# Retention and an ELU feed-forward network: units of 128 tokens of all heads in place of 256 tokens of four heads

## The chip, the cores and the metric

The kernel runs on one core of a Trainium2 chip. The metric is the device time in microseconds (us). Before the change the median of three runs is 307.68 us (306.76 to 308.19).

## The reference

Two layers follow each other. The first is retention: attention without a softmax, in which the score of a query for an earlier key is multiplied by a power of a decay that belongs to the head. The second is a feed-forward network with an ELU between its two products.

```python
# q, k, v: 8 batches, 8 heads, 576 tokens, 64 features, float32
scores = scale * np.matmul(q, k.transpose(0, 1, 3, 2))      # scale = 1 / 8
gamma  = 1.0 - 2.0 ** (-5.0 - np.arange(H))                 # one decay per head
rel    = pos[:, None] - pos[None, :]
Dmat   = np.where(rel >= 0, gamma ** rel, 0.0)              # causal
attn   = np.matmul(scores * Dmat, v)

x = attn.transpose(0, 2, 1, 3).reshape(8 * 576, 512)
h = x @ w_in                                                # 512 -> 2048
g = np.where(h > 0, h, np.exp(np.minimum(h, 0)) - 1)
out = g @ w_out                                             # 2048 -> 512, float32
```

Since `gamma ** (i - j)` is `gamma ** i * gamma ** -j`, the decay goes into q and k as a factor for each token and head, and the sum over all earlier tokens can be carried as a state, `k.T @ v`, a 64x64 block for each head.

## The kernel before, in words

**Units.** The first 512 tokens of a batch are worked in units, named by `seq` (L154): batch `b`, half `T` of 256 tokens, group `w` of four heads. That is 32 units, four to a batch. A tile holds two neighbouring tokens to a partition, so that a load's pieces are 512 bytes: `"h (p e) d -> p h (e d)"` with `e=2` (L167). The last 64 tokens of each batch go as a *rider* beside a unit (the functions whose name ends in `_rider`); a rider has one token to a partition and its loads (L379, L381) have pieces of 256 bytes.

**One unit.** `load` (L161) issues three DMAs from SP's queue. `cast` (L183) multiplies q and k by their factors, `gq` and `gk`, and turns them into bf16 (`cast_qk`, L178; `cast_v`, L181), mostly on POOL, that is GpSimd. `turn` (L202) transposes q and k by a DMA of SP's queue. Then come, all on PE with instructions that are recorded at L65:

- `scores` (L236): 16 matmuls on 64x64 quarters of the array, 128 columns each, into the PSUM tile `sc`. The two chunks `c` of a tile are 128 tokens each (64 partitions of two tokens).
- `masks` (L249): one DVE instruction that takes `sc` to bf16 and zeroes what isn't causal, into `pt` (L255).
- `inter` (L270): the states `s_first` and `s_mid`, as blocks for a pair of heads, times the queries, on the whole array, 128 columns each; four matmuls, or two in a first half, where no state is there for the first chunk.
- `values` (L280): 16 matmuls on 64x64 quarters, 128 columns each, into the PSUM tiles `x0` and `x1`.
- `state` (L305): 16 matmuls on 64x64 quarters, 64 columns each, into a free part of `x0` and `x1`.
- `prefix_mid` and `prefix_end` (L343, L348): two DVE instructions that add the chunk's state to the sum so far (L321, L323), and four POOL copies that put these sums as bf16 into `s_mid`, `s_first` or `s_last` (L355).
- `put_x` (L291): two ACT copies of the result into `xt`, the input of the feed-forward network (L297).

**Order.** Instructions keep the program's order on each engine (`pin`). `stretch(u)` (L432) works the unit's matmuls, and `inter`, `values` and `put_x` of the unit before it. The feed-forward network goes in jobs: `ffn1_half` (L514), eight matmuls of 256 columns, then on ACT an exponential and a Relu (L495, L498) and on DVE their combination (L499); and `ffn2` (L534), four matmuls of 512 columns, with a copy on ACT (L542) and a store from POOL's queue (L552) after the last four of a tile of tokens. `stage` (L789) runs these jobs in turn and calls `step` (L656) at places that are spread evenly over them. Each step casts and turns unit `u + 2`, loads unit `u + 4`, and works `stretch(u)`. The first eight units, the loads of the weights and the way into this order are written out by hand (L568 to L770).

Of the kernel before, what the change touches and what calls it, by code (L numbers as in the profile page):

```python
# [17 lines left out]
def kernel(  # L18
# [9 lines left out]
    nc = tc.nc  # L28
# [89 lines left out]
    s_mid = [const.tile([P, 2, P], BF16, name=f"s_mid{w}") for w in range(2)]  # L118
    s_first = [const.tile([P, 2, P], BF16, name=f"s_first{w}") for w in range(2)]
    s_last = [[const.tile([P, 2, P], BF16, name=f"s_last{o}{w}") for w in range(2)] for o in range(3)]  # L120
    for t in (*s_mid, *s_first, *s_last[0]):
        nc.vector.memset(t, 0.0)

    w_in_sb = const.tile([P, KJ, DF], BF16, name="w_in_sb")
# [36 lines left out]
    def load(u, last=False):  # L161
        b, T, w = seq[u]
        rqk = raw.tile([P, 2, 4, 2, D], FP32, name="rqk", tag="rqk")
        rv = raw.tile([P, 4, 2, D], FP32, name="rv", tag="rv", bufs=5)
        parts = [(rqk[:, 0], q), (rqk[:, 1], k), (rv, v)]
        for dst, src in parts[::-1] if last else parts:
            pin(nc.sync.dma_start(  # L167
                dst.rearrange("p h e d -> p h (e d)"),
                src[b, 4 * w : 4 * w + 4, 2 * P * T : 2 * P * (T + 1), :].rearrange("h (p e) d -> p h (e d)", e=2),
            ))  # L170
        rawt[u] = rqk, rv

    def cast_qk(u, i, eng, es=(0, 1)):
        b, T, w = seq[u]
        x = rawt[u][0][:, i].rearrange("p h e d -> p e h d")
        g = (gq, gk)[i][:, 2 * T : 2 * T + 2, 4 * w : 4 * w + 4].unsqueeze(3).to_broadcast([P, 2, 4, D])
        for e in es:
            pin(tt[eng](natt[u][0][:, i, e], x[:, e], g[:, e], ALU.mult))  # L178
# [54 lines left out]
    def half(i):  # L233
        return slice(i * D, (i + 1) * D)

    def scores(u):  # L236
        sc = ps_s.tile([P, 2, 512], FP32, name="sc", tag="sc")
        for hl in range(2):
            for ek in range(2):
                for i in range(2):  # L240
                    r = half(i)
                    for c in range(2):
                        cs = slice(c * C, (c + 1) * C)
                        o = (hl * 2 + ek) * P
                        mm(pairs(sc[cs, i, o : o + P]), trt[u][r, 4 + ek * 2 + hl, cs], queries(u, r, hl, c),
                           start=True, stop=True)
        score_ps[u] = sc

    def masks(u, hls=None):  # L249
        sc = score_ps[u]  # L250
        if u not in ptt:
            ptt[u] = ppool.tile([P, 2, 2, 2 * P], BF16, name="pt", tag="pt")
        m = mask.rearrange("p k e r -> p (k e r)").unsqueeze(1)
        if hls is None:
            pin(nc.vector.tensor_tensor(  # L255
                ptt[u].rearrange("p i h n -> p (i h) n"), sc.rearrange("p i (h n) -> p (i h) n", h=2),
                m.to_broadcast([P, 4, 2 * P]), ALU.mult,
            ))
        else:
            for hl in hls:  # L260
                pin(nc.vector.tensor_tensor(
                    ptt[u][:, :, hl], sc.rearrange("p i (h n) -> p i h n", h=2)[:, :, hl],
                    m.to_broadcast([P, 2, 2 * P]), ALU.mult,
                ))
# [5 lines left out]
    def inter(u, hls=(0, 1), to=None):  # L270
        b, T, w = seq[u]
        x = to or xps
        for c in range(2):
            if T + c == 0:
                continue
            s = s_mid[w] if c else s_first[w]
            for hl in hls:
                acc_x(c, 2, pairs(x[c][:, hl * P : (hl + 1) * P]), s[:, hl], queries(u, slice(0, P), hl, c), to)

    def values(u, hls=(0, 1), to=None):  # L280
        vn, pt = natt[u][1], ptt[u]
        x = to or xps
        for hl in hls:
            for e in range(2):
                for c in range(2):
                    cs = slice(c * C, (c + 1) * C)
                    for i in range(2):
                        acc_x(c, i, x[c][half(i), hl * P : (hl + 1) * P], vn[cs, 2 * hl + i, e],
                              pt[cs, i, hl, e * P : (e + 1) * P], to)

    def put_x(u, hls=(0, 1), to=None, eng="ss"):  # L291
        b, T, w = seq[u]
        h0, h1 = hls[0], hls[-1] + 1
        for c in range(2):
            src = (to or xps)[c][:, : 2 * P].rearrange("p (h e r) -> p h e r", h=2, e=2)[:, h0:h1]
            dst = xt_tile(b)[:, T, 2 * w + h0 : 2 * w + h1, c * P : (c + 1) * P].rearrange("p h (r e) -> p h e r", e=2)
            pin(engines[eng[c]](dst, src))  # L297
# [6 lines left out]

    def state(u, to=None):  # L305
        qkn, vn = natt[u]
        stt[u] = to or list(xps)
# [17 lines left out]
    def prefix(u, c, put):  # L325

        b, T, w = seq[u]
        before = mids[u] if c else total[w] if T else None
        new = rpool.tile([P, 2, D], FP32, name="end" if c else "mid", tag="end" if c else "mid")
# [12 lines left out]

    def prefix_mid(u, put="p"):  # L343
        prefix(u, 0, put)
# [15 lines left out]
    def put_end(u, eng="p"):  # L360
        blocks(s_end(u), total[seq[u][2]], eng)


    mask_t = const.tile([P, ST], BF16, name="mask_t")

    def mask_rider():
        pin(nc.vector.memset(mask_t, 1.0))
        for i in range(2):
            m = mask_t[half(i)]
            pin(nc.gpsimd.affine_select(out=m, in_=m, compare_op=ALU.is_ge, fill=0.0, base=0, pattern=[[1, ST]],  # L370
                                        channel_multiplier=-1))

    rawr, natr, trr, ptr, late = {}, {}, {}, {}, []

# [57 lines left out]
    def stretch(u, put="p"):  # L432
        old = u - 1 in natt and u - 1 in ptt
        rider = late.pop() if late else None
        new_x()
        if old:
            inter(u - 1)
        if rider is not None:
            inter_rider(rider)
        if u < NS:  # L440
            scores(u)
            masks(u)
# [6 lines left out]
        if u < NS:  # L449
            state(u)  # L450
        if old:
            put_x(u - 1)
            drop(u - 1)
        if rider is not None:
            put_rider(rider)
        if u < NS:
            prefix_mid(u, put)
            prefix_end(u, put)
        if u in rides:
            masks_rider(rides[u])  # L460
            late.append(rides[u])
# [111 lines left out]
    warm(7)  # L573
    cast(0, "v", "p", None)
    turn_pe(0, between=2)
    warm(2)
    cast(1, "v", "p", None)
    for u in range(FT - 1):
        scores(u)
        cast_v(u, "s")  # L580
        if u == 2:
            cast_v(3, "s")
        if u:
# [15 lines left out]
        if u == 1:  # L599
            cast(3, None, None, None)  # L600
            masks(1)
            turn_pe(2, "ss")
            prefix_mid(1)
            prefix_end(1)
            for t in (*s_last[1], *s_last[2]):
# [159 lines left out]
    finish(7)  # L765
    cast(10)
    turn(10)
    mask_rider()
    while half1:
        some()  # L770
    def mix(a, c):
# [82 lines left out]
```

## Time and profile before

| | |
|---|---|
| median of three runs | 307.68 us |
| lowest, highest | 306.76, 308.19 us |
| profiled execution | 306.73 us |
| its span (first to last instruction) | 305.0 us |
| mean granted clock of PE | 0.999 |
| busy: PE, ACT, POOL, DVE | 297.2, 212.5, 169.5, 165.2 us |
| DMA, mean over the span | 178 GB/s |

The profile is of one execution, and times in it count from the first instruction. A row of the timeline gives start, duration, engine, line of the kernel, operation, output and inputs, and how many neighbouring instructions it merges; the bracket behind it is the idle time of the engine before it and what ended that. A row of the grouped lines ends in busy time, mean duration in ns, and idle time before. In a row of stretches of time, the last three columns are the granted clock, the mean busy share of the 16 DMA engines, and the rate. That share counts a packet's whole time, so packets that overlap on an engine take it above 1. Matmuls are pipelined: the modelled end of one lies behind the start of the next, so the spacing of starts tells what each occupies.

### The profile page before, as it was taken

Reading aid. Unit: us, or ns where it says so; the run is one execution under the profiler, and the core shown is the slowest. Engines: PE = TensorE matmul, PEld = TensorE weight load, DVE = VectorE, ACT = ScalarE, POOL = GpSimd, SP = SyncE. Lnnn points to the kernel's source line nnn. Section 1 sums busy time; section 2 is a strip of 40 time slices with the busy share of each in tenths; the row PEclk is TensorE's granted clock in tenths of the full one; section 3 lists DMA queues with packets and bytes.
Section 4 is the critical chain, followed back from the end, with each engine's and each line's share of the span. In section 5 each row is a group of like instructions: output and inputs, shape, how many; then the busy total and the mean of one; then the engine's idle time right before and its main releaser. Section 6 shows DMA issues by size and latency. Waiting matters only on the chain.

```text
span 305.0 us, 8990 instructions
## 1 busy us (share of the span) xinstructions
PE 297.2 (97%) x3562; PEld 200.4 (66%) x3562; DVE 165.2 (54%) x306; ACT 212.5 (70%) x429; POOL 169.5 (56%) x373
## 2 busy tenths in 40 slices
PE   8889999999999999999999999999999999999995
PEld 5544457767766766777676676677766776666654
DVE  4866566667465556555653455555555555434430
ACT  4679857967766776677777677767776777677751
POOL 5888887787957575757370437584757530201000
PEclk9999999999999999999999999999999999999999
DMA  7999997999999888776944098667759301100112
GB/s 205 315 368 368 356 297 170 258 242 289 264 219 222 216 193 206 195 183 108 263 125 139 34 189 169 172 175 214 172 137 218 88 34 38 38 34 37 49 57 69
DMA packets 102187, 54.34 MB, mean 178 GB/s; under 512 B 46272, under 2 KB 95680, under 8 KB 102144
## 3 DMA queue, kind: packets, MB, share of 16 engines
q1 hardware_dynamic: 99392, 45.04, 63.2%
q0 software_dynamic: 2672, 8.65, 7.6%
q8 instruction: 28, 0.46, 0.6%
q14 instruction: 15, 0.12, 0.1%
q10 hardware_dynamic: 80, 0.07, 0.1%
HBM read 36.70 MB, written 9.44 MB: 151 GB/s over the span
## 4 chain that ended last, share of the span: by engine, by line
PE 82%; DMA 10%; SPq 3%; ACT 1%; DVE 1%; issue 1%; POOL 0%; DVEq 0%
PE pm L65 37%; PE ph L65 36%; DMA rqk<-in_moe_w_out_dram 5%; PE x L65 5%; PE sc L65 3%; SPq L167 3%; DMA rqk<-in_q_dram 2%; DMA rqk<-in_moe_w_in_dram 2%; PE pe L65 1%; DVE pt L255 1%; ACT ph L498 1%; SPq L145 1%; ACT e L495 1%; PE ptr L212 0%; DVE g L499 0%
## 5 line engine op out<-in xcount | busy, mean ns | idle before, releaser
L499 DVE SCALAR_TENSOR_TENSOR g<-e,ph 128x512 bf16<-128x512 f32 x128 | 88.0, 688 | 103.9 <-ACT ph L498 101.3
L65 PEld LDWEIGHTS <-w_in_sb 128*128 128x128 bf16 x1088 | 105.1, 98 | 42.6 <-DVE xt L297 0.5
L65 PE MATMUL pm<-w_out_sb,g 128*128 128x512 bf16 x512 | 131.9, 379 | 0.0
L65 PE MATMUL ph<-xt,w_in_sb 128*128 128x256 bf16 (+1 forms) x960 | 131.4, 280 | 0.1
L495 ACT ACTIVATE e<-ph 128x512 f32<-128x512 f32 x144 | 85.9, 596 | 58.4 <-PE ph L65 58.2
L498 ACT ACTIVATE ph<-ph 128x512 f32<-128x512 f32 x144 | 85.6, 594 | 0.0
L65 PEld LDWEIGHTS <-g 128*128 128x128 bf16 x512 | 48.7, 98 | 35.3
L355 POOL CAST s_mid<-mid 64x128 bf16<-64x128 f32 x64 | 18.6, 291 | 68.6 <-DVE mid L323 38.5
L552 POOL DMA_DIRECT2D out_dram<-ot x35 | 20.0, 574 | 37.5 <-ACT ot L542 31.1
L178 POOL TENSOR_TENSOR qkn<-rqk,gk 128x256 bf16<-128x256 f32 x64 | 37.8, 609 | 4.1 <-DMA rqk<-in_k_dram 3.7
L255 DVE TENSOR_TENSOR pt<-sc,mask 128x1024 bf16<-128x1024 f32 x30 | 36.5, 1218 | 0.7 <-PE sc L65 0.5
L178 POOL TENSOR_TENSOR qkn<-rqk,gq 128x256 bf16<-128x256 f32 x51 | 30.2, 610 | 2.5 <-DMA rqk<-in_q_dram 0.8
L297 ACT CAST xt<-x 128x256 bf16<-128x256 f32 x62 | 23.6, 454 | 9.6 <-PE x L65 9.4
L542 ACT COPY ot<-pm 128x512 f32<-128x512 f32 x35 | 20.5, 589 | 9.5 <-PE pm L65 9.0
L499 DVE SCALAR_TENSOR_TENSOR gt<-e,ph 128x512 bf16<-128x512 f32 x16 | 11.0, 688 | 14.8 <-ACT ph L498 14.8
L65 PE MATMUL ph<-xtail,w_in_sb 128*128 128x256 bf16 x128 | 16.6, 273 | 0.0
L181 POOL CAST vn<-rv 128x512 bf16<-128x512 f32 x23 | 13.9, 602 | 0.0
L65 PE MATMUL sc<-qkT 64*64 64x128 bf16 x512 | 13.3, 222 | 0.0
L65 PE MATMUL x<-pt,vn 64*64 64x128 bf16 x496 | 12.3, 217 | 0.0
L65 PE MATMUL pm<-w_out_sb,gt 128*128 128x512 bf16 x48 | 11.8, 379 | 0.0
L355 POOL CAST s_first<-end 64x128 bf16<-64x128 f32 x32 | 9.9, 311 | 1.7
L65 PEld LDWEIGHTS <-qkT 64*64 64x64 bf16 x512 | 8.2, 106 | 4.1 <-ACT qkT L213 0.9
(77 smaller groups left out, 190.6 us busy)
## 6 DMA issues: line engine op xcount, KB each, us to landing
rqk<-in_q_dram SPq DMA_DIRECT2D x32, 256.0 KB, 3.9
rqk<-in_k_dram SPq DMA_DIRECT2D x32, 256.0 KB, 4.5
rv<-in_v_dram SPq DMA_DIRECT2D x32, 256.0 KB, 5.1
out_dram<-ot POOLq DMA_DIRECT2D x31, 256.0 KB, 3.9
rqk<-in_moe_w_in_dram SPq DMA_DIRECT2D x16, 256.0 KB, 5.7
rqk<-in_moe_w_out_dram SPq DMA_DIRECT2D x16, 256.0 KB, 5.6
rqt<-in_q_dram SPq DMA_DIRECT2D x8, 128.0 KB, 4.8
rqt<-in_k_dram SPq DMA_DIRECT2D x8, 128.0 KB, 5.0
```

The source lines that it names most:

```text
L65: pin(nc.tensor.matmul(*a, **kw))
L167: pin(nc.sync.dma_start(dst.rearrange("p h e d -> p h (e d)"), src[b, 4 * w : 4 * w + 4, 2 * P * T : 2 * P * (T + 1), :].rearrange("h (p e ...
L178: pin(tt[eng](natt[u][0][:, i, e], x[:, e], g[:, e], ALU.mult))
L181: pin(engines[eng](natt[u][1], rawt[u][1]))
L255: pin(nc.vector.tensor_tensor(ptt[u].rearrange("p i h n -> p (i h) n"), sc.rearrange("p i (h n) -> p (i h) n", h=2), m.to_broadcast([P, 4, ...
L297: pin(engines[eng[c]](dst, src))
L355: pin(engines[eng](dst[half(i), :, half(i)], src[half(i)]))
L495: pin(nc.scalar.activation(e, ph, AF.Exp))
L498: pin(nc.scalar.activation(ph, ph, AF.Relu))
L499: pin(nc.vector.scalar_tensor_tensor(dst, view(e), -1.0, view(ph), ALU.add, ALU.min))
L542: pin(nc.scalar.copy(ot, pm))
L552: pin((queue or nc.gpsimd).dma_start(dst, src))
```

## The change

From the third batch on (`fine(u)`, 24 units) a unit is 128 tokens of all eight heads, one token to a partition. The number of units stays: `t = u % 4` names the quarter of the 512 tokens. The two chunks of a unit are 64 tokens each.

- The loads bring pieces of 256 bytes, one head and token each (`"h p d -> p h d"`).
- `cast_qk` is one instruction of 512 elements for q and one for k, with tables of their own, `gqf` and `gkf`, that `tables()` makes at the start, together with `mask_t`, which was made later before. `cast_v` moves behind the stretch.
- `scores` and `values` are 16 matmuls each, of 64 columns; `inter` has one for each of four head pairs and each chunk, of 64 columns. `state` writes into the free half of `sc`, right behind `scores`.
- `masks` is one instruction of 512 elements. The states are added in two instructions of 256 elements (`prefix_fine`) and copied to bf16 by two POOL instructions, which take both chunks at once. At a batch's last unit these two take one chunk, and two more go to `s_last`.
- `s_mid` and `s_first` become parts of one tile, `s_fine[0]`, beside a second, `s_fine[1]`.

The core of the diff:

```diff
+    s_fine = [const.tile([P, 2, HP, P], BF16, name=f"s_fine{o}") for o in range(2)]
+    s_mid, s_first = [[s_fine[0][:, n, 2 * w : 2 * w + 2] for w in range(2)] for n in range(2)]
...
+    def fine(u):
+        return seq[u][0] >= 2
...
     def load(u, last=False):
+        if fine(u):
+            t = u % 4
+            for dst, src in parts:
+                pin(nc.sync.dma_start(
+                    dst.rearrange("p a e d -> p (a e) d"), src[b, :, t * P : (t + 1) * P, :].rearrange("h p d -> p h d"),
+                ))
...
     def cast_qk(u, i, eng, es=(0, 1)):
+        if fine(u):
+            pin(tt[eng](
+                natt[u][0][:, i].rearrange("p e h d -> p (e h) d"), rawt[u][0][:, i].rearrange("p a e d -> p (a e) d"),
+                (gqf, gkf)[i][:, u % 4].unsqueeze(2).to_broadcast([P, H, D]), ALU.mult,
+            ))
...
+    fines = [(m, i, c) for m in range(HP) for i in range(2) for c in range(2)]
     def scores(u):
+        if fine(u):
+            for m, i, c in fines:
+                cs, r = half(c), half(i)
+                mm(sc[cs, i, m * C : (m + 1) * C], trt[u][r, HP + m, cs], trt[u][r, m, cs],
+                   start=(m == 0), stop=True, skip_group_check=True)
...
     def masks(u, hls=None):
+        if fine(u):
+            pin(nc.vector.tensor_tensor(
+                ptt[u], sc[:, :, : HP * C].rearrange("p i (m n) -> p i m n", m=HP),
+                mask_t.unsqueeze(1).unsqueeze(1).to_broadcast([P, 2, HP, C]), ALU.mult,
+            ))
...
     def inter(u, hls=(0, 1), to=None):
+        if fine(u):
+            for c in range(2):
+                if u % 4 + c == 0:
+                    continue
+                s = s_fine[u % 2][:, 0] if c else s_fine[(u - 1) % 2][:, 1]
+                for m in range(HP):
+                    acc_x(c, 2, x[c][:, m * C : (m + 1) * C], s[:, m], trt[u][:, m, half(c)])
...
     def values(u, hls=(0, 1), to=None):
+        if fine(u):
+            for m, i, c in fines:
+                acc_x(c, i, x[c][half(i), m * C : (m + 1) * C], vf[half(c), 2 * m + i], pt[half(c), i, m])
...
     def state(u, to=None):
+        if fine(u):
+            for m, i, c in fines:
+                o = HP * C + m * D
+                mm(score_ps[u][half(i), c, o : o + D], kf[half(c), 2 * m + i], vf[half(c), 2 * m + i],
+                   start=False, stop=True, skip_group_check=True)
...
+    def prefix_fine(u):
+        new = rpool.tile([P, 2, HP, D], FP32, name="run", tag="run", bufs=2)
+        before = total["f"] if u % 4 else None
+        for c in range(2):
+            sum_into(new[:, c], score_ps[u][:, c, HP * C :].rearrange("p (m d) -> p m d", m=HP), before)
+            before = new[:, c]
+        total["f"] = before
+        ends = u % 4 == 3
+        for i in range(2):
+            k = 1 if ends else 2
+            pin(nc.gpsimd.tensor_copy(s_fine[u % 2][half(i), :k, :, half(i)], new[half(i), :k]))
+        if ends:
+            blocks(s_lasts[u // 4 % 3], before, "p")
...
     def stretch(u, put="p"):
             scores(u)
+            if fine(u):
+                state(u)
             masks(u)
...
     def step():
-            cast(u + 2)
+            cast(u + 2, v=None)
             turn(u + 2)
...
         stretch(u)
+        if 8 < u < NS - 2:
+            cast_v(u + 2, "p")
...
+    def tables():
+        pin(nc.vector.memset(mask_t, 1.0))
+        pin(nc.gpsimd.iota(pf_i, pattern=[[P, FT]], base=-MID, channel_multiplier=1))
+        for c in range(2):
+            m = mask_t[half(c)]
+            pin(nc.gpsimd.affine_select(out=m, in_=m, compare_op=ALU.is_ge, fill=0.0, base=0, pattern=[[1, C]],
+                                        channel_multiplier=-1))
+        pin(nc.vector.memset(s_fine[1], 0.0))
+        pin(nc.vector.tensor_copy(pf, pf_i))
+        pin(nc.vector.tensor_tensor(
+            ef, pf.unsqueeze(2).to_broadcast([P, FT, H]), lgt.unsqueeze(1).to_broadcast([P, FT, H]), ALU.mult,
+        ))
...
     turn_pe(0, between=2)
+    tables()
...
         if u == 0:
+            pin(nc.scalar.activation(gqf, ef, AF.Exp, bias=bq))
+            pin(nc.scalar.activation(gkf, ef, AF.Exp, bias=bk, scale=-1.0))
```

More of the change, by code (lines that the diff above doesn't have):

```diff
@@ L116 @@
                                         pattern=[[2, C]], channel_multiplier=-2)
[L118 to L121, printed above, removed]
+    mask_t = const.tile([P, ST], BF16, name="mask_t")
+    pf_i = const.tile([P, FT], I32, name="pf_i")
+    pf = const.tile([P, FT], FP32, name="pf")
+    ef = const.tile([P, FT, H], FP32, name="ef")
+    gqf = const.tile([P, FT, H], FP32, name="gqf")
+    gkf = const.tile([P, FT, H], FP32, name="gkf")
+    s_fine = [const.tile([P, 2, HP, P], BF16, name=f"s_fine{o}") for o in range(2)]
+    s_mid, s_first = [[s_fine[0][:, n, 2 * w : 2 * w + 2] for w in range(2)] for n in range(2)]
+    s_lasts = [const.tile([P, HP, P], BF16, name=f"s_last{o}") for o in range(3)]
+    s_last = [[t[:, 2 * w : 2 * w + 2] for w in range(2)] for t in s_lasts]
+    for t in (s_fine[0], s_lasts[0]):
         nc.vector.memset(t, 0.0)
@@ L251, in masks @@
         if u not in ptt:
-            ptt[u] = ppool.tile([P, 2, 2, 2 * P], BF16, name="pt", tag="pt")
+            ptt[u] = ppool.tile([P, 2, HP, C] if fine(u) else [P, 2, 2, 2 * P], BF16, name="pt", tag="pf" if fine(u) else "pt")
+        if fine(u):
[3 more added lines that the diff above has]
+            ))
+            return
         m = mask.rearrange("p k e r -> p (k e r)").unsqueeze(1)
@@ L328, in prefix @@
         before = mids[u] if c else total[w] if T else None
-        new = rpool.tile([P, 2, D], FP32, name="end" if c else "mid", tag="end" if c else "mid")
+        new = rpool.tile([P, 2, D], FP32, name="end" if c else "mid", tag="end" if c else "mid", bufs=3)
         st = state_ps(u, c)
@@ L361, in put_end @@
         blocks(s_end(u), total[seq[u][2]], eng)
[L364 to L371, printed above, removed]
     rawr, natr, trr, ptr, late = {}, {}, {}, {}, []
@@ L448, in stretch @@
             values_rider(rider)
-        if u < NS:
+        if u < NS and not fine(u):
             state(u)
@@ L456, in stretch @@
         if u < NS:
[L457 to L458 removed]
+            if fine(u):
+                prefix_fine(u)
+            else:
+                prefix_mid(u, put)
+                prefix_end(u, put)
         if u in rides:
@@ L604 @@
             prefix_end(1)
-            for t in (*s_last[1], *s_last[2]):
+            for t in s_lasts[1:]:
                 pin(nc.vector.memset(t, 0.0))
```

16 lines of the change are left out of this document (15 added, 1 removed).

## The prediction, as it was made before the result

> **What bounds the kernel now.** First the engines' busy shares and the slices of the profile page:
>
> ```profile
> span 305.0 us, 8990 instructions
> PE 297.2 (97%) x3562; PEld 200.4 (66%) x3562; DVE 165.2 (54%) x306; ACT 212.5 (70%) x429; POOL 169.5 (56%) x373
> PE   8889999999999999999999999999999999999995
> DMA  7999997999999888776944098667759301100112
> PE 82%; DMA 10%; SPq 3%; ACT 1%; DVE 1%; issue 1%; POOL 0%; DVEq 0%
> ```
>
> PE is the bound: 97% busy, 82% of the chain that ended last, and a 9 in every slice after the third. The DMA engines are the second resource: their row stands at 6 to 9 in most slices up to the 31st. Now one stretch in the timeline (columns: start, duration, engine, line, operation, count), from the last feed-forward job ahead of it to the first behind it:
>
> ```profile
> 153.13 1.03 PE L65 MATMUL pm<-w_out_sb,g 128*128 128x512 bf16 x4
> 153.99 0.28 PE L65 MATMUL x<-qkT,s_first 128*128 128x128 bf16 x2
> 154.10 0.28 PE L65 MATMUL x<-qkT,s_mid 128*128 128x128 bf16 x2
> 154.22 0.28 PE L65 MATMUL x<-qkTt,s_last 128*128 128x64 bf16 x4
> 154.43 0.42 PE L65 MATMUL sc<-qkT 64*64 64x128 bf16 x16
> 154.67 0.39 PE L65 MATMUL x<-pt,vn 64*64 64x128 bf16 x16
> 154.90 0.23 PE L65 MATMUL x<-ptt,vt 64*64 64x64 bf16 x8
> 154.96 0.30 PE L65 MATMUL x<-vn,qkn 64*64 64x64 bf16 x16
> 155.19 1.05 PE L65 MATMUL ph<-xt,w_in_sb 128*128 128x256 bf16 x8
> ```
>
> The starts have no hole, so whatever a group occupies from its start to the next start is time of the kernel. The whole attention of a unit costs about 1.2 us there (153.99 to 155.19, a rider included), and only this can be saved on PE; the feed-forward jobs stay as they are.
>
> **Matmuls of the 24 new units.** Batches 2 to 7 have four units each, before and after. Per unit, `scores` and `values` keep 16 matmuls on 64x64 tiles, but each streams 64 columns where it streamed 128. Before, scores took 154.67 - 154.43 = 0.24 us and values 154.90 - 154.67 = 0.23. The price of the new form stands two rows on: the rider's 8 matmuls of 64 columns on 64x64 tiles took 154.96 - 154.90 = 0.06, so 16 take 0.12. Saved: 0.12 + 0.11 = 0.23 us a unit, 24 x 0.23 = 5.5 us. `state` keeps its 16 matmuls of 64 columns and only moves ahead of `values`, at no price, since both stand between the same two changes of tile size.
>
> `inter` goes from matmuls of 128 columns, one for each pair of heads in a unit of four heads, to 64 columns over all four pairs. Four of the old ones took 154.22 - 153.99 = 0.23. The rider's four of 64 columns took 154.43 - 154.22 = 0.21, but a change of tile size is in that. It can be taken out by a unit of a first half, which has only two old ones:
>
> ```profile
> 176.91 0.28 PE L65 MATMUL x<-qkT,s_mid 128*128 128x128 bf16 x2
> 177.12 0.42 PE L65 MATMUL sc<-qkT 64*64 64x128 bf16 x16
> ```
>
> Two old ones and the change take 0.21, so the change is 0.21 - 0.115 = 0.095, and four new ones are 0.115: half of the old price, in proportion to the columns. Per batch, old: 2 + 2 + 4 + 4 = 12 of 0.0575 = 0.69 us; new: 4 + 8 + 8 + 8 = 28 of 0.029 = 0.81. Added: 0.12 x 6 = 0.7 us. On PE the change is worth 5.5 - 0.7 = **4.8 us**.
>
> The Trainium skill ("TensorE: Matmul & The Clock Gate", section "Wait — 56ns, not 53.3ns?") says that two matmuls never start less than about 25 ns apart, however few columns they have; by that 16 would take 0.40 us and each halved block would become longer, not shorter. The rider's 8 matmuls in 0.06 us disagree, 8 ns apart, on four 64x64 tiles in turn; on the full array the 29 ns fits it.
>
> **The other engines.** Rows of the grouped lines:
>
> ```profile
> L255 DVE TENSOR_TENSOR pt<-sc,mask 128x1024 bf16<-128x1024 f32 x30 | 36.5, 1218 | 0.7 <-PE sc L65 0.5
> L261 DVE TENSOR_TENSOR pt<-sc,mask 128x512 bf16<-128x512 f32 x4 | 2.7, 686 | 0.5 <-PE sc L65 0.5
> L323 DVE TENSOR_TENSOR end<-x,mid 128x128 f32<-128x128 f32 x28 | 8.2, 292 | 4.0 <-POOL s_mid L355 0.5
> L355 POOL CAST s_mid<-mid 64x128 bf16<-64x128 f32 x64 | 18.6, 291 | 68.6 <-DVE mid L323 38.5 <-DVE mid L321 28.1
> L178 POOL TENSOR_TENSOR qkn<-rqk,gk 128x256 bf16<-128x256 f32 x64 | 37.8, 609 | 4.1 <-DMA rqk<-in_k_dram 3.7
> L181 POOL CAST vn<-rv 128x512 bf16<-128x512 f32 x23 | 13.9, 602 | 0.0
> ```
>
> DVE: the mask goes from 1.22 to 0.69 us; the two sums of 128 elements (0.29 each) become two of 256, between 0.29 and the 0.69 of 512 elements; in proportion 0.42 each. A unit needs 1.80 before and 1.53 after. POOL: four casts of q and k at 0.61 become two of twice the width, between 0.61 and 1.22 each; the four copies into the state blocks at about 0.29 become two of 64x512, which I take at the 0.60 of the 512-element cast. Both come out even or lower. All of it lies under PE, and what its cover is worth shows where POOL's last copy for unit 9 meets PE's next need of it:
>
> ```profile
> 73.01 0.63 POOL L355 CAST s_first<-end 64x128 bf16<-64x128 f32 x2
> 74.04 0.28 PE L65 MATMUL x<-qkT,s_mid 128*128 128x128 bf16 x2
> ```
>
> The new copies start only after both sums, since one copy takes both states: mask and sums end at the old mask's start + 1.53 instead of + 1.80, and two copies take 1.2 instead of 1.3. So they end no later than the old ones at 73.64, 0.4 us before the need. Were each copy 0.9 us, PE would wait 0.2 us there. `cast_v` moves on POOL behind these copies, which lets the transposing DMA of the same step go 0.6 us sooner; its result is wanted two steps later. In the start, `tables` adds to DVE two memsets, a cast and a product, to POOL an iota and two selects, to ACT two small exponentials. They fall into these waits:
>
> ```profile
> 7.47 0.76 DVE L178 TENSOR_TENSOR qkn<-rqk,gq 128x256 bf16<-128x256 f32 x2 [1.87 <-DMA rqk<-in_q_dram]
> 8.40 1.19 POOL L178 TENSOR_TENSOR qkn<-rqk,gk 128x256 bf16<-128x256 f32 x2 [2.44 <-DMA rqk<-in_k_dram]
> 8.61 0.59 ACT L213 COPY qkT<-ptr 128x512 bf16<-128x512 bf16 x1 [1.05 <-PE ptr L212]
> ```
>
> The like instructions of the old start:
>
> ```profile
> L122 DVE MEMSET s_mid<- 128x128 uint32 x2 | 0.3, 165 | 0.0
> L370 POOL TENSOR_SCALAR_AFFINE_SELECT mask_t<-mask_t 64x64 bf16<-64x64 bf16 x2 | 0.5, 236 | 0.0
> L103 ACT ACTIVATE gq<-expo,bq 128x32 f32<-128x32 f32 x1 | 0.3, 322 | 0.8 <-DVE expo L96 0.8
> ```
>
> DVE's larger memset is four of the first row, 0.66 us, about 1.0 with the rest, in a wait of 1.87; POOL's selects 0.5 in 2.44; ACT's exponentials 0.64 in 1.05. I cost them at nothing; without the waits they would be 1 us, once.
>
> **The loads.** This is the part that can spoil it. A new unit loads the same 768 KB, but in pieces of 256 B (64 floats of one head and token) where the old ones were 512 B: 3072 pieces, not 1536. Only the rider loads (1536 pieces of 256 B) show that size. Stretches of the trace (last two columns: DMA share, GB/s):
>
> ```profile
> 158.00:163.50 5.50, 5.50 (x39) 3.67 (x38) 2.75 (x4) 3.60 (x8) 0.58 (x1) 1.00 0.64 194
> 165.50:167.50 2.00, 2.00 (x16) 1.31 (x14) 1.06 (x2) 1.41 (x4) 0.01 (x1) 1.00 0.34 131
> 178.00:184.50 6.50, 6.50 (x74) 4.31 (x76) 3.78 (x7) 4.73 (x10) 3.89 (x9) 1.00 0.96 244
> 210.00:216.00 6.00, 6.00 (x42) 3.89 (x41) 3.99 (x8) 4.34 (x10) 3.42 (x8) 1.00 0.96 240
> 228.50:234.00 5.50, 5.50 (x86) 4.07 (x85) 3.09 (x5) 3.38 (x7) 4.38 (x10) 1.00 0.92 254
> 42.00:48.00 6.00, 5.89 (x85) 3.44 (x84) 5.21 (x11) 3.77 (x8) 4.66 (x12) 1.00 1.20 291
> 62.00:154.00 92.00, 92.00 (x1215) 64.31 (x1214) 53.06 (x91) 64.94 (x133) 63.07 (x138) 1.00 0.97 215
> ```
>
> The first moves one unit and one store: 5.50 x 0.64 = 3.52 us of all 16 engines. The second is a store alone: 0.68. So a unit in 512-B pieces costs 2.84 us, 16 x 2.84 / 1536 = 29.5 ns a piece. The next three each move a unit, a store and a rider: 6.24, 5.76 and 5.06 us; less 3.52 the rider costs 2.72, 2.24 and 1.54 us, or 28, 23 and 16 ns a piece. I take the middle one: 3072 x 23.3 / 16 = 4.5 us for a new unit, 1.6 more; ends 3.1 and 5.7 (the last at the old price of a piece).
>
> The Trainium skill ("DMA: Bandwidth & Descriptors") has two rules for this size. Its "Specifications" want 512 B for line rate, with a read-modify-write below; if that doubled a unit, it would be at the upper end. "Why small descriptors are slow (HBM only)" counts 11 cycles for 256 B, against 19 for 512 B by the same sum, so 16% more: 3.3 us as an estimate. The three rider rows lie between the two.
>
> From 62 to 154 us the share is 0.97 already, and 42 to 48 shows what the engines sustain when load follows load: 1.20 (a share above 1 means packets that overlap). 13 new units load in those 92 us: 13 x 1.6 = 21 us, 0.23 of share, 1.20 in all. So the DMA just keeps pace, and has no reserve. Loads run four units ahead, and the tightest place is early, at unit 10:
>
> ```profile
> 64.56 3.18 SPq L202 DMA_TRANSPOSE qkT<-qkn  x1
> qkT<-qkn SPq DMA_TRANSPOSE x1, 6.7
> 74.25 0.42 PE L65 MATMUL sc<-qkT 64*64 64x128 bf16 x16
> ```
>
> Unit 10's transposing DMA is issued at 64.6, lands 6.7 us later at 71.3, and its scores start at 74.25: 2.9 us to spare. Ahead of it in SP's queue and on the engines stand three new loads (units 9, 10, 11), up to 3 x 1.6 = 4.8 us more; the engines idle in part between, so I take about 3.9, a wait of **1.0 us** on PE (0 to 5.6 by the ends). Later units have more room.
>
> **Sum.** -4.8 + 1.0 = -3.8 us. The profiled execution took 306.73 us (span 305.0), so 302.9; the median of the three runs is 307.68, 0.95 above it, so **303.9 us**.
>
> **Rivals.** (1) The DMA engines become the bound. If a piece of 256 B costs as much as one of 512 B, 29.5 ns, a unit costs 2.84 us more, 13 of them 37 us, and the share wanted is 0.97 + 0.40 = 1.37 against 1.20: 92 us of work then take 105, 13 us late. Less 4.8 on PE, that is 307.7 + 8.2 = 315.9, slower. It decides from where the lag reaches 4.8 us: share 1.263, 27 us over 13 units, 2.07 us a unit, 25.6 ns a piece. For it: the rider at 28 ns and the 1.20. Against: the riders at 16 and 23 ns, and the reserve of four units, which swallows the first microseconds of lag. (2) The same in part: at 25 to 27 ns the two cancel, 307.7 or so. (3) The short matmuls do not run at the riders' pace. At 25 ns each, 32 of them take 0.80 us, not 0.47: 24 x 0.33 = 8 us longer, 315.7 us. Against it stand the 64-column rows above, so it gets little.
>
> **How the numbers follow.** Forecast 0.62 (302 to 306); rival 1 0.22; rival 2 0.12; rival 3 0.04. A difference under 0.5%, 306.1 to 309.2 us, is what a measurement of this kernel can't tell from no change: faster 0.62, same 0.12, slower 0.26. The range starts at 302.0 (no wait for loads gives 302.9, and the three runs before reach 0.9 below their median) and goes up to 315.0, which takes in rival 2 and most of rival 1. The forecast's own range is 302 to 306.
>
> **What would show it.** In the profile after: 16 score matmuls in 0.12 us from start to next start; `inter` of a unit in 0.23; a stretch some 0.2 us shorter; PE still without holes after 76 us. A unit's load read in the same way at 3.1 to 5.7 us. Wrong would be PE waiting on `qkn` or `qkT` behind a load at many stretches, with a DMA share above 1.2 over 62 to 154 us: rival 1. Wrong in the other term: score starts 25 ns apart.

## The result, and the profile after

| | before | after |
|---|---|---|
| median, us | 307.64 (306.33 to 309.65, 22 runs) | 306.0 (303.76 to 310.33, 22 runs) |
| ratio, 95% interval | | 0.9943 [0.9924, 0.9961] |
| span of the profiled execution, us | 305.0 | 306.8 |

The kernel became faster by 0.6%, 1.7 us, where 3.8 us (1.2%) were forecast. Medians and ranges here and below are of all executions, ratios leave out those more than 1.5% above the fastest of their kernel, and the profiled execution of the changed kernel, 308.53 us, is one of these, as is that of the run with only the units from 12 on in large pieces. A second profile of the same kernel, of 305.52 us, is used beside it (the first experiment).

From the page of the changed kernel, and its stretches of time (the last three columns are granted clock, DMA share, GB/s):

```profile
span 306.8 us, 9084 instructions
PEclk9999999997999999999999999999999999999999
```

```profile
62.00:154.00 92.00, 89.48 (x1240) 61.78 (x1238) 48.90 (x88) 62.46 (x130) 58.28 (x86) 0.98 1.21 210
```

PE had no idle time between 62 and 154 us; now 2.5 us are missing there, and the granted clock dips in the tenth slice. The DMA share is 1.21, where 1.20 was forecast. The longest row in the list of PE's waits after 50 us (the others are of 0.3 us or less) and PE's timeline name one place:

```profile
PE x L65 <- POOL s_fine L421: 2.4, 1, 2.4
```

```profile
69.05 1.04 PE L65 MATMUL ph<-xt,w_in_sb 128*128 128x256 bf16 x8
72.47 0.29 PE L65 MATMUL x<-qkT,s_fine 128*128 128x64 bf16 x4 [2.39 <-POOL s_fine L421]
72.69 0.32 PE L65 MATMUL sc<-qkT 64*64 64x64 bf16 x16
72.84 0.30 PE L65 MATMUL sc<-vn,qkn 64*64 64x64 bf16 x16
72.97 0.30 PE L65 MATMUL x<-pt,vn 64*64 64x64 bf16 x16
73.20 1.64 PE L65 MATMUL pm<-w_out_sb,g 128*128 128x512 bf16 x4
```

In stretch 9, the one that works unit 9's scores, PE stands 2.39 us, because `inter` of unit 8, the first of the new form, waits for POOL's copy of the state. Four matmuls of 512 columns then take 1.64 us, where four such took 1.03 at 153.13 us in the kernel before. POOL's timeline says why the copy is late:

```profile
66.18 1.04 POOL L197 TENSOR_TENSOR qkn<-rqk,gqf 128x512 bf16<-128x512 f32 x1 [3.45 <-DMA rqk<-in_q_dram]
67.32 1.04 POOL L197 TENSOR_TENSOR qkn<-rqk,gkf 128x512 bf16<-128x512 f32 x1
69.99 0.61 POOL L208 CAST vn<-rv 128x512 bf16<-128x512 f32 x1 [1.63 <-DMA rv<-in_v_dram]
70.54 0.58 POOL L630 DMA_DIRECT2D out_dram<-ot  x1
71.12 1.29 POOL L421 CAST s_fine<-run 64x512 bf16<-64x512 f32 x2
```

The copies' input came from DVE:

```profile
67.06 0.42 DVE L390 TENSOR_TENSOR run<-sc,run 128x256 f32<-128x256 f32 x1
```

So the state stood ready at 67.5, but POOL works in program order and had the three casts of unit 10 ahead of the copies. These waited 3.45 and 1.63 us for load 10, and the copies ended at 72.41. Before, on POOL and PE:

```profile
62.20 1.19 POOL L178 TENSOR_TENSOR qkn<-rqk,gq 128x256 bf16<-128x256 f32 x2 [0.54 <-DMA rqk<-in_q_dram]
64.47 0.61 POOL L181 CAST vn<-rv 128x512 bf16<-128x512 f32 x1
66.47 0.62 POOL L355 CAST s_mid<-mid 64x128 bf16<-64x128 f32 x2 [0.39 <-DVE mid L321]
68.79 0.28 PE L65 MATMUL x<-qkT,s_mid 128*128 128x128 bf16 x2
```

The casts stood in the same order, but they waited only 0.54 us for load 10, and the copy ended at 67.09, 1.7 us ahead of its need. That reserve was the cover, and the late load 10 used it up; the experiments show how far its 256-B pieces are the cause.

The granted clock (the third number from the right), in stretches of 1 us behind the wait:

```profile
74.00:75.00 1.00, 1.00 (x4) 0.45 (x3) 0.65 (x2) 0.12 (x1) 0.79 (x2) 0.50 1.16 319
75.00:76.00 1.00, 1.00 (x7) 0.69 (x6) 0.00 (x0) 0.00 (x0) 0.94 (x2) 0.50 1.27 284
77.00:78.00 1.00, 1.00 (x8) 0.66 (x7) 0.23 (x1) 0.73 (x2) 0.98 (x2) 1.00 1.41 226
```

With the clock of 0.75 in the stretch before these and of 0.55 from 76 to 77 us, the missing clock is 0.25 + 0.5 + 0.5 + 0.45 = 1.7 us.

A stretch farther on is nearly as forecast:

```profile
94.81 0.40 PE L65 MATMUL x<-qkT,s_fine 128*128 128x64 bf16 x8
95.14 0.32 PE L65 MATMUL sc<-qkT 64*64 64x64 bf16 x16
95.29 0.30 PE L65 MATMUL sc<-vn,qkn 64*64 64x64 bf16 x16
95.41 0.30 PE L65 MATMUL x<-pt,vn 64*64 64x64 bf16 x16
95.65 1.05 PE L65 MATMUL ph<-xt,w_in_sb 128*128 128x256 bf16 x8
```

By starts: `inter` and the change of tile size 0.33, scores 0.15, state 0.12, values and the change 0.24, in all 0.84 us, where a like stretch before (200.04 to 201.05) took 1.01. The time from the start of `inter` to the next feed-forward job, summed over the 25 stretches behind 60 us, fell from 25.07 to 21.48 us (the wait lies ahead of `inter`'s start): **3.6 us** saved on PE, not 4.8.

### The profile page after: what moved, and what is told of

Read it like the earlier page. It is cut to its first block, busy times and chain, and to the rows that moved or that the text cites. A ratio compares the mean times of both kernels' runs of the same rounds, so it can differ in the third digit from the quotient of the medians.

```text
span 306.8 us, 9084 instructions
## 1 busy us (share of the span) xinstructions
PE 295.2 (96%) x3658; PEld 197.8 (64%) x3658; DVE 159.7 (52%) x303; ACT 210.3 (69%) x431; POOL 167.7 (55%) x290
## 4 chain that ended last, share of the span: by engine, by line
PE 78%; DMA 12%; SPq 3%; ACT 3%; issue 1%; POOL 1%; DVE 1%; ACTq 0%
PE pm L65 36%; PE ph L65 34%; DMA rqk<-in_moe_w_out_dram 6%; PE x L65 4%; PE sc L65 3%; SPq L188 3%; DMA rv<-in_v_dram 3%; DMA rqk<-in_q_dram 2%; DMA rqk<-in_moe_w_in_dram 2%; ACT e L573 1%; PE pe L65 1%; ACT ph L576 1%; SPq L153 1%; ACT xt L357 0%; POOL s_fine L421 0%
## 5 line engine op out<-in xcount | busy, mean ns | idle before, releaser
L421 POOL CAST s_fine<-run 64x512 bf16<-64x512 f32 (+1 forms) x48 | 26.6, 555 | 61.5 <-DVE run L390 58.2
L197 POOL TENSOR_TENSOR qkn<-rqk,gqf 128x512 bf16<-128x512 f32 x24 | 25.3, 1053 | 4.1 <-DMA rqk<-in_q_dram 3.5
L197 POOL TENSOR_TENSOR qkn<-rqk,gkf 128x512 bf16<-128x512 f32 x24 | 25.1, 1046 | 0.1
L353 ACT CAST xt<-x 128x256 bf16<-128x256 f32 x48 | 15.5, 377 | 9.2 <-PE x L65 9.2
L390 DVE TENSOR_TENSOR run<-sc,run 128x256 f32<-128x256 f32 x42 | 17.7, 420 | 0.8
L291 DVE TENSOR_TENSOR pt<-sc,mask_t 128x512 bf16<-128x512 f32 x24 | 16.4, 684 | 1.2 <-PE sc L65 1.2
L65 PEld LDWEIGHTS <-s_fine 128*128 128x128 bf16 x192 | 9.8, 98 | 7.2 <-POOL s_fine L421 2.7
L65 PE MATMUL x<-qkT,s_fine 128*128 128x64 bf16 (+1 forms) x188 | 11.3, 196 | 2.6 <-POOL s_fine L421 2.4
L205 POOL TENSOR_TENSOR qkn<-rqk,gk 128x256 bf16<-128x256 f32 x16 | 9.5, 612 | 3.7 <-DMA rqk<-in_k_dram 3.3
```

The lines of the kernel that those rows point to most:

```text
L65: pin(nc.tensor.matmul(*a, **kw))
L197: pin(tt[eng](natt[u][0][:, i].rearrange("p e h d -> p (e h) d"), rawt[u][0][:, i].rearrange("p a e d -> p (a e) d"), (gqf, gkf)[i][:, u % ...
L291: pin(nc.vector.tensor_tensor(ptt[u], sc[:, :, : HP * C].rearrange("p i (m n) -> p i m n", m=HP), mask_t.unsqueeze(1).unsqueeze(1).to_broa ...
L353: pin(engines[eng[c]](xt_tile(b)[:, T, :, o : o + C], xps[c][:, : HP * C].rearrange("p (m n) -> p m n", m=HP)))
L390: pin(nc.vector.tensor_tensor(dst, a, b, ALU.add))
L421: pin(nc.gpsimd.tensor_copy(s_fine[u % 2][half(i), :k, :, half(i)], new[half(i), :k]))
```

## The experiments

Theory A: the saving on PE is 3.6 us, and what is missing of it is lost at the hand-over to the new units, at 57 to 76 us. Theory B: the denser loads cost something all along the kernel. Theory C: the additions in the start cost more than nothing.

**The same kernel again.**

> The changed kernel once more, for a second profile. Theory A (a late load holds up POOL, and PE waits behind it at one place): PE stands idle once after 60 us, for 1 to 2.5 us ahead of the inter matmuls of the second stretch of new units (about 70 us), released by POOL's copy into s_fine, which stood behind cast_v of unit 10 and its load; no other wait of PE over 0.3 us after 60 us. Time 306.0. Theory B (the DMA engines are full over the whole middle): further waits of PE for qkT or qkn between 80 and 230 us. Theory C (the start): the first matmul of the feed-forward network later than 18.55 us by 0.2 us or more, and by 50 us PE 1 us behind the kernel before.

305.53 us (303.19 to 308.51), 0.9914 [0.9885, 0.9943]. The list of PE's waits, and POOL's timeline:

```profile
PE x L65 <- POOL s_fine L421: 1.4, 1, 1.4
```

```profile
65.35 1.04 POOL L197 TENSOR_TENSOR qkn<-rqk,gqf 128x512 bf16<-128x512 f32 x1 [3.08 <-PE sc L65]
68.63 0.61 POOL L208 CAST vn<-rv 128x512 bf16<-128x512 f32 x1 [1.10 <-DMA rv<-in_v_dram]
69.77 1.30 POOL L421 CAST s_fine<-run 64x512 bf16<-64x512 f32 x2
```

The same wait at the same place, 1.4 us, without the dip behind it. (The first releaser is named PE; in the other profile it is the load of q.) But this execution has a dip of the clock at its start, worth 1.1 us (the last section), and with it the spans add up: 305.0 - 3.6 + 1.4 + 1.1 = 303.9, measured 303.8. For the first profile the like sum, 305.0 - 3.6 + 2.4 + 1.7 = 305.5, falls 1.3 us short of its span; 1.0 of that lies ahead of the hand-over (the start, below).

**Unit 10's cast of v behind the copies.**

```diff
-    cast(10)
+    cast(10, v=None)
...
-        if 8 < u < NS - 2:
+        if 8 <= u < NS - 2:
             cast_v(u + 2, "p")
```

> cast_v of unit 10 moved on POOL from ahead of unit 8's stretch to behind it, as it stands for all later units; the loads stay as they are. Theory A: POOL's copies into s_fine for unit 8 no longer stand behind the v of load 10; they wait only for q and k of load 10, so PE's wait at the second stretch falls from 2.4 us to under 0.8, and PE's clock stays up: 303.0 to 304.0 us. Theory B: the load is as late as before and PE waits for it elsewhere; 306. Theory C: 306.

304.67 us (302.88 to 306.36), 0.9904 [0.9872, 0.9935]. The wait at `s_fine` is gone, and another has come a step later:

```profile
76.39 0.32 PE L65 MATMUL sc<-qkT 64*64 64x64 bf16 x16 [0.90 <-DMA qkT<-qkn]
```

These are unit 10's scores, the place that the prediction had named, at about its price: 0.90 us idle, forecast 1.0. The interval overlaps that of the unchanged order, so no gain is shown: load 10 is late whichever of its users comes first.

**All loads in 512-B pieces.** The computation is the new one, but each new unit is loaded in the old pattern, which puts other data into the tiles.

```diff
-        if fine(u):
+        if False:
             t = u % 4
```

> The changed kernel, but the loads of the new units take the old pattern, 512-byte pieces, two tokens to a partition of four heads; the data then stand in other places than the matmuls take them for. Same bytes, half the pieces. Theories A and B: no wait at the second stretch, DMA share over 62 to 154 us back from 1.21 to about 0.97, and what is left is PE's gain of 3.6 us (read from the stretches): 304.0 us. Theory C: still 1 us of loss at the start: 305.0.

303.6 us (303.03 to 304.52), 0.9875 [0.9852, 0.9897].

```profile
62.00:154.00 92.00, 90.83 (x1317) 64.44 (x1329) 51.02 (x94) 64.92 (x135) 61.97 (x93) 1.00 1.01 217
```

No wait over 0.3 us is left after 50 us (the 1.2 us that PE seems idle here are gaps of 0.16 with the releaser "issue", where records are missing), and the share is back at 1.01. This is what the rest of the change is worth, 307.3 - 303.6 = 3.7 us (3.2 to 4.5 by the interval), as the trace says of PE. So the smaller pieces cost some 2 us in this kernel, 305.53 - 303.6. The interval overlaps a little with that of the repeat (0.9885 to 0.9943), and not with that of the first set (0.9924 to 0.9961).

**The old kernel with the new loads.** Units 8 to 31 of the kernel before, loaded in 256-B pieces (other data in the tiles).

```diff
+        if b >= 2:
+            t = u % 4
+            for dst, src in parts:
+                pin(nc.sync.dma_start(
+                    dst.rearrange("p a e d -> p (a e) d"), src[b, :, t * P : (t + 1) * P, :].rearrange("h p d -> p h d"),
+                ))
```

> The kernel before with the new units' loads alone: from the third batch on, the same bytes in 256-byte pieces, which puts other data into the places that the old matmuls read. Theory A: POOL stands at the v of load 10 in this kernel too, ahead of unit 8's copies; a wait of 1 to 3 us at the second stretch, 309 to 311 us. Theory B: the same or more, with waits at several places: 311 or above. Theory C: no change, 307.6.

307.83 us (306.44 to 308.68), 1.0011 [0.9991, 1.003]: in the old kernel the same loads cost nothing that shows. The stretches and POOL:

```profile
62.00:154.00 92.00, 90.84 (x1203) 64.30 (x1213) 53.17 (x91) 65.00 (x133) 63.08 (x137) 1.00 1.22 218
```

```profile
63.69 1.18 POOL L186 TENSOR_TENSOR qkn<-rqk,gq 128x256 bf16<-128x256 f32 x2 [1.84 <-DMA rqk<-in_q_dram]
67.62 0.62 POOL L363 CAST s_mid<-mid 64x128 bf16<-64x128 f32 x2
```

The DMA share is as in the changed kernel, and POOL waits 1.84 us for load 10 here too. The copy of `s_mid` ends at 68.24, 0.74 us ahead of its need at 68.98. From the first cast of unit 10 to the end of the copies pass 4.55 us here, and 71.07 - 65.35 = 5.72 in the repeat of the changed kernel. The larger terms of this 1.2 us are that one pair of copies (1.30 us, not 0.62) now carries both states, 0.68 more, and the wait for v, 1.10; the `mask_t` selects, 0.5, are gone from there. That, and a load 10 that came 1 us later against PE, is the difference between a reserve of 0.74 and a wait of 1.39. So the new loads alone bring no wait, and the new computation alone (all loads in 512-B pieces) brings none: it takes both. Why load 10 came later is not settled: in the traces its three issues from SP end at 62.06 us here and at 63.79 in the repeat.

**Only units 8 to 11 in 512-B pieces, and only the units from 12 on.** `if fine(u):` in `load` becomes `if fine(u) and u >= 12:` and `if fine(u) and u < 12:`, again with other data in the tiles that are loaded in the old pattern.

> The changed kernel, but units 8 to 11 (the third batch, the first of the new form) are loaded in the old pattern of 512-B pieces; units 12 to 31 stay in 256-B pieces. The data of batch 2 therefore stand in other places of the tiles. Theory A (the loss lies in the hand-over alone: loads 9 to 11 land late, POOL stands at a cast that waits for load 10, and the copies of s_fine behind it come late): the wait of 1.4 to 2.4 us near 71 us goes although the later units' loads stay as they are; about 303.6 us, as with all loads in 512-B pieces, with a DMA share of about 1.15 over 62 to 154 us. Theory B (the denser loads cost something all along the kernel, in small pieces that no single row shows): most of the loss stays, 305 to 305.7 us.

> The converse of the last: units 8 to 11 in 256-B pieces as in the changed kernel, units 12 to 31 in 512-B pieces, so the data of batches 3 to 7 stand in other places of the tiles. Theory A: the wait at 71 us stays at 1.4 to 2.4 us and nothing is won, 305.3 to 306 us, though the DMA share over 80 to 154 us falls to about 1.0. Theory B: 303.6 to 304.3 us.

304.27 us, 0.9876 [0.9849, 0.9903] with the first four in large pieces; 305.81 us, 0.9905 [0.987, 0.994] with all the others in large pieces. PE's longest wait after 50 us and the stretch from 62 to 154 us, in the first and then in the second:

```profile
PE x L65 <- POOL s_fine L437: 0.3, 1, 0.3
```

```profile
62.00:154.00 92.00, 90.79 (x1277) 64.28 (x1292) 50.89 (x93) 65.46 (x136) 62.05 (x94) 1.00 1.21 216
```

```profile
PE x L65 <- POOL s_fine L421: 1.8, 1, 1.8
```

```profile
62.00:154.00 92.00, 88.78 (x1235) 62.52 (x1246) 48.87 (x88) 63.26 (x132) 58.43 (x86) 0.98 1.02 213
```

The intervals overlap; the profiles tell the two apart: a DMA share of 1.21 without the wait at the hand-over, and a share of 1.02 with a wait of 1.8 us there and the dip behind it. And with dense loads from unit 12 on the time is that of all loads in large pieces (0.9876 and 0.9875). So it is not the density over the kernel that costs, but four loads at the hand-over. Theory B falls.

**The loads ahead of the transposing DMAs.** First for units 9, 10 and 11, without and with the later cast of v; then for 10 and 11 alone, again without and with it.

```diff
-    turn(7)
     load(9)
+    turn(7)
...
-    turn(8)
     load(10)
+    turn(8)
...
-    turn(9)
     load(11)
+    turn(9)
```

> The changed kernel with one thing moved: in SP's queue each of the loads of units 9, 10 and 11 stands ahead of the transposing DMA that it stood behind (of units 7, 8 and 9). Theory A with SP's queue as the cause of the late landing: load 10 is issued 2 to 3 us sooner, POOL's cast of unit 10 waits under 1.5 us, s_fine comes in time, 303.6 to 304.3 us. Theory A' (the DMA engines are full there, the order in the queue only changes who is late): the wait moves to the transposing DMAs of units 8 or 9, and the time stays at 305 to 306 us.

> The last kernel, and the cast of v of unit 10 on POOL moved behind the copies of s_fine of unit 8 (as in the second run). Theory A: the two remedies take away both waits that were seen, at s_fine near 71 us and at the scores of unit 10 (0.9 us); 303.3 to 304.0 us, no wait of PE over 0.3 us after 60 us. Theory A': one wait of 0.5 to 1.5 us stays at the scores of unit 8, 9 or 10; 304.5 to 305.3 us.

> The changed kernel with the loads of units 10 and 11 ahead of the transposing DMAs of units 8 and 9 in SP's queue; the load of unit 9 stays behind the transposing DMA of unit 7, which was late (1.4 to 1.5 us at 57 us) when all three loads were moved. Theory A (single late transfers and casts at the hand-over, each of them to be cured by the order of issue): the wait at 57 us is gone, unit 10 is cast before the copies of s_fine are due, 303.6 to 304.3 us, no wait of PE over 0.5 us after 50 us. Theory A' (the DMA engines are full there, so one transfer or another is always late): a wait of 1 us or more shows at unit 8, 9 or 10; 305 to 306 us.

> The last kernel and the cast of v of unit 10 behind the copies of s_fine of unit 8. Theory A: as the last or up to 0.3 us better, 303.4 to 304.0 us, the same as with all loads in 512-B pieces. Theory A': 304.8 to 305.5 us with a wait of 1 us or so at the scores of unit 8, 9 or 10.

305.29 us, 0.9916 [0.9887, 0.9946]; 305.45 us, 0.9917 [0.9894, 0.994]; 306.17 us, 0.9965 [0.9945, 0.9985]; 305.95 us, 0.9962 [0.994, 0.9984]. PE's timeline in the first, and (two rows) in the third:

```profile
57.26 0.42 PE L65 MATMUL sc<-qkT 64*64 64x128 bf16 x16 [1.39 <-DMA qkT<-qkn]
```

```profile
65.14 0.32 PE L65 MATMUL sc<-qkT 64*64 64x64 bf16 x16 [0.60 <-DMA qkT<-qkn]
72.13 0.32 PE L65 MATMUL sc<-qkT 64*64 64x64 bf16 x16 [1.97 <-DMA qkT<-qkn]
```

Each order takes away the wait at `s_fine` and makes another transfer late: unit 7's transposing DMA (1.39 and 1.54 us), or those of units 8 and 9 (in the fourth 0.62 and 1.04 us). Theory A, that the right order takes the loss away, expected 303.3 to 304.3 us; none of the four came there. A', that one transfer or another is late there in any order, had the waits right in kind (it named units 8 to 10, not 7), and three of the four medians lie 0.15 to 0.45 us above its ranges. Its reason, that the DMA engines are full, was not told apart from late issues in SP's queue. No order tried gives back the 2 us.

**Scores and values issued twice.**

```diff
-            for m, i, c in fines:
+            for m, i, c in fines + fines:
```

> The changed kernel with the scores and the values matmuls of each new unit issued twice (the values are then added twice into the result, which the time doesn't depend on). It measures the price of the 16 short matmuls by itself. If a group costs 0.12 us as predicted and the 0.03 more seen in the trace is paid once, at the change between tile sizes: scores 0.15 + 0.12 = 0.27 from start to next start, values and change 0.24 + 0.12 = 0.36, 24 x 0.24 = 5.8 us more in all. If each such matmul is dearer than predicted (9.4 ns apart, not 7.5): scores 0.30, values 0.39, 24 x 0.30 = 7.2 us more.

The values are then added twice into the result, so it differs. One execution, 313.26 us; a stretch of it:

```profile
93.86 0.45 PE L65 MATMUL sc<-qkT 64*64 64x64 bf16 x32
94.13 0.30 PE L65 MATMUL sc<-vn,qkn 64*64 64x64 bf16 x16
94.26 0.48 PE L65 MATMUL x<-pt,vn 64*64 64x64 bf16 x32
94.67 1.05 PE L65 MATMUL ph<-xt,w_in_sb 128*128 128x256 bf16 x8
```

Scores 0.27: the first 16 cost 0.15, the next 0.12, so 0.03 goes once to the entry into the small tiles. Values 0.41, 0.17 more than the 0.24 of a single set, where 0.12 or 0.15 was expected; in the other stretches without a rider they take 0.37 or 0.38 as a rule, 0.14 more. So a second set of values costs a little more than one of scores, and why is open. The price of a single set in the middle of the run stands in the changed kernel, where a rider's eight follow it:

```profile
111.07 0.30 PE L65 MATMUL x<-pt,vn 64*64 64x64 bf16 x16
111.19 0.24 PE L65 MATMUL x<-ptt,vt 64*64 64x64 bf16 x8
```

That is 0.12, where at the end of the run 0.24 - 0.095 leaves 0.145.

**The change from the fourth batch on.** Units 8 to 11 keep the old form and their large pieces.

```diff
     def fine(u):
-        return seq[u][0] >= 2
+        return seq[u][0] >= 3
```

> The change from the fourth batch on instead of the third: units 8 to 11 keep the old form with loads in 512-B pieces, units 12 to 31 take the new form with loads in 256-B pieces. Five batches of new units save 5/6 of the 3.6 us seen on PE, 3.0 us. Theory A (the loss is made where PE, POOL and the DMA queue run with the least reserve, at units 8 to 11, and units from 12 on have more, as the run with units 8 to 11 in 512-B pieces showed): no wait at 70 to 90 us, 307.5 - 3.0 = 304.5 us, 304.1 to 304.8. Theory A' (the loss comes with the first new unit, wherever it stands): a wait of 1 us or more moves with it to about 85 to 92 us, 305.5 to 306.5 us.

**304.13 us** (303.84 to 304.7), 0.9872 [0.9839, 0.9905], four executions, shorter than those of both kernels; against the repeat of the change (0.9914 [0.9885, 0.9943], in another set of runs) the intervals still overlap a little, against the first set (0.9943 [0.9924, 0.9961]) they don't. Stretch and waits of PE:

```profile
62.00:154.00 92.00, 92.00 (x1253) 64.12 (x1251) 51.77 (x92) 65.37 (x135) 61.65 (x103) 1.00 1.19 211
```

```profile
PE x L65 <- POOL s_fine L437: 0.3, 1, 0.3
```

PE is full from 62 to 154 us, with a share of 1.19, and the row of 0.3 us is its longest wait after 50 us. So the wait doesn't move with the first new unit. The 25 stretches sum to 22.11 us, 3.0 less than before, which is 5/6 of 3.6.

## Why the prediction was right or wrong

The gain came to less than half of the forecast, and two terms of the sum were mis-sized: the saving on PE (3.6 us for 4.8), and the loss to late loads (2.0 for 1.0).

**Matmuls, -4.8 us: right in kind, too large.** The 64-column matmuls run near the rider's pace, and the rival of 25 ns has no part in it: `inter` takes the 0.33 us forecast with its change (0.23 + 0.095), and `state` 0.12. But the price for `scores` and `values`, 0.12 each, was read from a rider's eight matmuls, which stand in the middle of a run of 64x64 work. At the two ends of that run, next to the full array, a set costs up to 0.03 more. Over the 25 stretches `scores` went from 5.95 to 3.52 us, a saving of 2.4 where 2.9 were forecast; `values` and `state`, with the riders' values, from 11.44 to 9.35, 2.1 for 2.6; and `inter`, with its change, from 7.20 to 8.11, a cost of 0.9 for 0.7. So -4.8 becomes -3.6.

**The other engines: here the working failed.** The prices were right or near: the mask 0.684 us, the sums 0.42, the copies 0.61 each, the q and k casts 1.05, at the upper half of the stated bounds. The step that failed is "they end no later than the old ones". It was made for unit 9's copies, from DVE's times and the copies' own. (The row beside it was also misread: `inter` at 74.04 reads `s_mid`, whose copy ended at 72.95, not the `s_first` shown. The new copies carry both states, so the 0.4 us stand.) On POOL the copies stand behind casts that wait for a load, and the working of the loads followed load 10 only into SP's queue and the transposing DMA, not into POOL's queue. There it stops the copies for unit 8, one unit earlier than the place named: they ended at 72.41 and 71.07 us in the two profiles, and PE waited 2.39 and 1.39 us for them.

**Loads: the price of the pieces right, the place and size of the loss wrong.** The share was to rise from 0.97 to 1.20 and rose to 1.21, or 0.24 x 92 / 13 = 1.7 us a unit for the 1.6 forecast (1.4 against the 1.01 of the run in large pieces). The working had a slip: its cheapest rider row gives 3.1 us a unit, which does not lie between 3.3 and 5.7. Nor is 1.20 the most that the share can reach: from 77 to 78 us it is 1.41. "PE still without holes after 76 us" holds. The wait of 1.0 us at unit 10's scores did come, at 0.90, when the other was moved out of its way. In the changed kernel as it stands the wait is 1.4 to 2.4 us in stretch 9, and in the longer of the two profiles the dip of the clock adds 1.7. The run with all loads in large pieces puts the loss at about 2 us in the median.

**The start at nothing: open.** The first feed-forward matmul starts at 18.55 and 18.89 us in the two profiles with the old start, and at 18.43 to 19.45 in the twelve with the new. But at the scores of unit 7 PE is later in every new profile. These scores, before and in the first profile after, and a wait that only the latter has:

```profile
54.22 0.42 PE L65 MATMUL sc<-qkT 64*64 64x128 bf16 x16
```

```profile
44.75 0.81 PE L239 MATMUL ptr<-ident,qkn 128*128 128x128 bf16 x8 [0.62 <-DVE mid L388]
55.24 0.42 PE L65 MATMUL sc<-qkT 64*64 64x128 bf16 x16
```

These scores start at 54.22 and 54.40 us with the old start; with the new at 54.73 to 55.24 in the four without a dip at the start, the one above included, and at 55.09 to 56.12 in the six with one (two more have a wait at this very place). So profiled executions lose 0.3 us or more ahead of the hand-over. The medians don't show it (3.7 us with large pieces, where PE saves 3.6), but their interval leaves room for 0.4, and what causes it was not tested: theory C is not settled.

**Sum.** Forecast -4.8 + 1.0; measured -3.6 + 2.0, so -1.6 of the -1.7 us. The 2.0 is a difference of medians; the two profiles show 1.4 us, and 4.1 with the dip. Rival 1, the DMA engines as the bound of the whole stretch, did not come: the share reaches 1.2 and PE waits nowhere behind the hand-over. Rival 2 is what it looks like in the median, a saving of which more than half is cancelled, but by its price it needed dearer pieces than were seen. That a loss came near the place named, and not far from its size, was in part luck: it came by a path that the working didn't have.

## What to carry to other kernels

A late transfer is to be followed into every queue in which an instruction waits for it: what counts is what stands behind that instruction, here a copy on POOL that had nothing to do with the load. A denser transfer costs where the reserve is smallest, here where the kernel passes from one scheme to the next. So look for room before the new scheme begins: with one batch in six left in the old form the wait was gone, and the time, as far as the intervals tell, was shorter in spite of the smaller saving. Read the price of a short matmul at the edge of its run, not from its middle.

## What the runs showed of the hardware

The granted clock of PE falls to 0.50 behind some short waits, and not behind others of the same length. Behind the 2.39 us above it cost 1.7 us, and as much behind 1.84 us in the run with only the units from 12 on in large pieces; behind 1.78 us in the run with doubled matmuls, 1.97 us in the third order of the loads and the 1.4 us of the repeat there was no dip. At the start PE waits 0.81 us for a mask, and the first feed-forward matmuls follow; the repeat (with its stretch from 18 to 20 us), and then the first profile after:

```profile
17.88 0.43 PE L65 MATMUL st<-pt,vn 64*64 64x128 bf16 x8 [0.81 <-DVE pt L304]
18.43 1.06 PE L65 MATMUL ph<-xt,w_in_sb 128*128 128x512 bf16 x2
```

```profile
18.00:20.00 2.00, 2.00 (x23) 0.82 (x23) 0.88 (x2) 0.47 (x2) 2.00 (x4) 0.50 1.06 388
```

```profile
18.42 0.31 PE L65 MATMUL st<-pt,vn 64*64 64x128 bf16 x8 [0.81 <-DVE pt L304]
18.78 0.59 PE L65 MATMUL ph<-xt,w_in_sb 128*128 128x512 bf16 x2
```

The same wait of 0.81 us is followed by a dip in one execution and by none in the other, so the wait alone doesn't decide it; what does is open. From the first of these matmuls to the scores of unit 4 pass 42.30 - 18.43 = 23.87 us with the dip, 41.28 - 18.55 = 22.73 before: 1.1 us. It shows in 7 of the 12 profiles of kernels with the new start and in neither of the 2 with the old one. Yet a mean clock under 0.996, which any dip can cause, stands with 14 of 71 executions with the old start too, and with 30 of 92 with the new. Whether `tables` makes it more frequent stays open; by an estimate from these counts the difference of 13 in 100 would be worth 0.15 us.
